# A fused local-attention and gated-MLP kernel on one core: the fourth unit in Strassen's stays, joined groups for it, softmax steps on GpSimd

## The chip, the cores and the metric

One core of a Trainium2 chip runs the whole program: TensorE (PE in the profile; PEld its weight loads), VectorE (DVE), ScalarE (ACT), GpSimd (POOL) and SyncE (SP), whose queue issues all of this kernel's DMAs. The metric is the device time in microseconds of one launch; lower is better.

## The reference

```python
q, k, v: (4, 8, 768, 64) float32      # batch, heads, sequence, head dim
scores = q @ k.T / 8
is_global = pos_k < n_global          # n_global = 8
is_local  = 0 <= pos_q - pos_k < n_local   # n_local = 96
dist = where(is_global & ~is_local, n_local, |pos_q - pos_k|)
scores = where(is_global | is_local, scores - slopes[h] * dist, -1e9)
a = exp(scores - max(scores))
a = a / (sum(a) + 1e-9)
x = (a @ v)                           # -> (3072 tokens, 512)
out = ((x @ w_a) * (x @ w_b)) @ w_out # w_a, w_b: (512, 1536); w_out: (1536, 512)
```

Each query sees at most 96 local keys and 8 global ones. The MLP has two first layers that are multiplied with each other, and a second layer.

## The kernel before

**Units, head pairs, feature pairs.** The 3072 tokens are six units of 512 tokens (0 to 5). A unit's attention is done in four head pairs of two heads ("granules", `granule_ops`, L648), each with four blocks of 128 queries. The 1536 features are six feature pairs (0 to 5) of 2 x 128 features. Each unit must meet each feature pair: 36 unit-and-pair passes of the MLP.

**Precision.** Every float32 operand of the MLP is split into a high and a low half in fp32r (`hh`/`hl`, `split`, L520), and each product is three matmuls: high x high, high x low, low x high. The weights arrive as raw words and are first converted (`to32`, L452: two ACT and four DVE operations on 128x512 a piece, six pieces a feature pair).

**Plain and Strassen.** `project_plain` (L1035) makes a pair's first layers of a unit with four products of 12 matmuls, 512 columns wide. `project` (L1095) does the same by Strassen's scheme with seven products of 12 matmuls, 256 wide; it needs sums and differences of the weight blocks (`convert`, L542, which writes them to DRAM, and `load_w`, L579, which reads and splits them) and of the blocks of X (`forms`, L906: four subtractions and seven splits; the plain `plain_forms`, L967, has four splits). The second layer (`back`, L1164, matmuls L1178) is 24 matmuls of 512 columns into four banks `acc` either way.

**Stays.** Only some feature pairs' weights fit in SBUF at a time. `STAYS` (L49) is the list of stays: which pairs are resident, which units come past in which order, and whether the stay is plain. `PASSES` (L57) is that list flattened. When the unit changes, the four `acc` banks are evicted and added to the unit's partial sums in DRAM (`evict`, L1195), and the next unit's X is loaded (`load_x`, L954) and put in forms, unless it has just come out of the attention.

**Attention of a granule.** PE makes the scores (L709, small 64x64 tiles), DVE adds the mask and reduces the minimum (L677), ACT takes exp and the sums (L693), DVE adds 1e-9 to the sums (L772) and takes reciprocals (L779), DVE or ACT scales (L792, L789), DVE transposes in 32x32 blocks (L808), a DMA writes the result to DRAM (`mir`) and eight DMAs bring it back rearranged as `px` and `py` (`carry`, L856), and PE makes the values (L341, or L322 in joined groups). Unit 0 (`DIRECT`) transposes on PE instead (L826, L827). There is one buffer each of `px`, `py` and `tt`, two of `t`, `vt` and `qk`.

Three ways exist to place the values. Unit 0 makes them at once. Units in `LAGGED` (1, 2, 3) make them after the next granule's scores, as a group of 32 matmuls of their own, and the scores in two groups of 24. Units in `JOINED` (4, 5) make all 48 score matmuls of a granule and the values of the granule before it (64 matmuls on 64x64 tiles, `parts`, L313) in one uninterrupted group on PE (`joined`, L726), which takes four PSUM banks. `NEAR` (0 to 3) are the units whose x is written straight into the tile X; the others' goes to DRAM through `vt` and is loaded when its pass comes.

**The order.** All operations go into a planner (`Schedule`, L160 on): each has a due time, costs per engine (`pe=`, `dve=`, `act=`, `pool=`), what it reads and writes, and the order of each engine's queue is fixed at build time by a list schedule over these. `SPANS` (L58) says over which stretch of passes (as positions in `PASSES`) a unit's attention is spread, `CONV` (L60) the same for the conversion of a feature pair's weights to Strassen's forms. Engines work through their queues in order, so an operation that waits holds up what stands behind it.

**The start.** `build` (L1535) loads the token counts, the table of positions and the first two granules' q and k, computes a flag, branches on it (the other side is a general, slow path that does not run here) and enters the planned program, whose first DVE work turns the table into distances and then into one mask per head (`masks`, L592).

## Time and profile before

| what | us |
|---|---|
| median of 3 runs | 723.44 |
| lowest and highest of them | 718.98, 724.59 |
| the profiled execution | 722.86 |
| its span, from first to last instruction | 721.0 |
| granted TensorE clock, mean | 0.990 |

The profiled execution is the one that all rows below come from. The span is what the rows show; 1.86 us lie around it. Rows of groups give the line of the kernel, the engine, the operation, output and input tiles with their sizes, the count, the time in which at least one of them ran, the mean length of one in ns, the idle time of the engine just in front of them, and what ended it. Rows of windows give a stretch of the span and each engine's busy time in it with the number of instructions, then the granted clock, the busy share of the 16 DMA engines and GB/s. Rows of the chain give start, length and work of what each step of the chain that ended last waited for.

### The profile page before, as it was taken

To read this page: it belongs to the slowest core of one execution; us is meant where nothing else is said; L and a number is where in the kernel's file an instruction comes from. 1 tells how busy PE (TensorE), PEld (TensorE's weight loads), DVE (VectorE), ACT (ScalarE), POOL (GpSimd) and SP (SyncE) were. 2 spreads that over 40 slices of the span, in tenths; PEclk is the share of its full clock that TensorE was granted. 3 is DMA by queue.
4 is the path that set the end of the run, shared out by engine and by line. 5 is a ranking of instruction groups with operands and counts; after the bars stand their busy time and mean duration, and the time that the engine had idled before them with its cause. 6 is when DMAs were issued, how large, how long until landed. Compare 5 with 4: busy or idle time off the path is not lost.

```text
span 721.0 us, 15565 instructions
## 1 busy us (share of the span) xinstructions
PE 685.9 (95%) x5808; PEld 602.3 (84%) x5808; DVE 581.6 (81%) x1552; ACT 384.9 (53%) x988; POOL 1.8 (0%) x8
## 2 busy tenths in 40 slices
PE   5598999999999999999999999999999999999995
PEld 4487877777777888888999998999898999999994
DVE  7999897878697776899899997999988558646652
ACT  5988675845565674566554546566434434424220
POOL 1000000000000000000000000000000000000000
PEclk9889999999999999999999999999999999999998
DMA  8547888998989997776786888748893423533121
GB/s 299 190 165 284 252 270 294 314 287 285 293 295 293 264 322 250 255 243 213 260 295 234 302 262 282 261 161 275 292 293 142 132 81 97 160 117 103 59 75 63
DMA packets 67910, 162.43 MB, mean 225 GB/s; under 512 B 8433, under 2 KB 21873, under 8 KB 66033
## 3 DMA queue, kind: packets, MB, share of 16 engines
q1 hardware_dynamic: 67824, 161.34, 67.7%
q8 instruction: 48, 0.79, 0.4%
q14 instruction: 38, 0.30, 0.1%
HBM read 110.45 MB, written 50.86 MB: 224 GB/s over the span
## 4 chain that ended last, share of the span: by engine, by line
PE 70%; DVE 13%; DMA 10%; ACT 4%; issue 2%; SPq 0%; ACTq 0%; DVEq 0%
PE acc L1178 22%; PE al L1001 16%; PE ga L1001 12%; PE ps L709 4%; DMA wr<-wts 3%; PE pa L341 3%; DMA qk<-qk 2%; DMA wl_A<-dw_A 1%; DVE t L677 1%; DVE tt L808 1%; DMA X<-dx 1%; DVE t L792 1%; DVE wm L495 1%; PE ps_al L322 1%; ACT wm L470 1%
## 5 line engine op out<-in xcount | busy, mean ns | idle before, releaser
L1178 PE MATMUL acc<-w_O,hh 128*128 128x512 f32 x576 | 197.0, 400 | 0.0
L1178 PEld LDWEIGHTS acc<-w_O,hh 128*128 128x128 f32 x576 | 108.3, 188 | 24.9 <-issue 1.5
L1178 PE MATMUL acc<-w_O,hl 128*128 128x512 f32 x288 | 113.7, 395 | 0.8 <-DVE hl L443 0.8
L693 ACT ACTIVATE t<-t,sm 128x168 f32<-128x168 f32 x192 | 81.1, 425 | 15.7 <-DVE sm L677 15.6
L1001 PE MATMUL al<-xf_T,w_S 128*128 128x256 f32 x576 | 76.7, 283 | 0.7 <-ACT s L433 0.7
L1001 PEld LDWEIGHTS al<-xf_T,w_S 128*128 128x128 f32 x576 | 72.4, 189 | 1.4 <-ACT s L433 0.9
L1178 PEld LDWEIGHTS acc<-w_O,hl 128*128 128x128 f32 x288 | 54.3, 188 | 10.8 <-DVE hl L443 1.4
L433 ACT CAST hh<-h 128x512 fp32r<-128x512 f32 (+1 forms) x61 | 36.0, 592 | 48.2 <-DVE h L443 23.6
L470 ACT ACTIVATE wm<-wr 128x512 f32<-128x512 f32 x54 | 36.2, 671 | 42.6 <-DMA wr<-wts 25.5
L709 PEld LDWEIGHTS ps<-qk 64*64 64x64 f32 x1056 | 32.8, 141 | 26.7 <-issue 14.0
L433 ACT COPY s<-al 128x512 f32<-128x512 f32 x44 | 25.7, 584 | 54.0 <-PE al L1001 53.8
L443 DVE TENSOR_TENSOR hl<-h,hh 128x512 fp32r<-128x512 f32 (+1 forms) x78 | 49.8, 644 | 4.9 <-ACT hh L433 4.5
L709 PE MATMUL ps<-qk 64*64 64x104 f32 (+2 forms) x1056 | 39.3, 276 | 14.5 <-DMA qk<-qk 7.1
L677 DVE CUSTOM_DVE_ANT_0 t<-ps,mask 128x168 f32<-128x168 f32 x176 | 48.6, 326 | 3.2 <-PE ps L709 3.0
L1110 DVE TENSOR_TENSOR s<-ga,s 128x512 f32<-128x512 f32 x48 | 32.8, 684 | 15.2 <-PE ga L1001 15.0
L808 DVE STREAM_TRANSPOSE tt<-t 128x512 f32<-128x512 f32 x80 | 40.9, 553 | 1.2 <-DMA mir<-tt 0.6
L1001 PE MATMUL ga<-xf_T,w_S 128*128 128x256 f32 x288 | 38.5, 283 | 1.1 <-DVE s L1110 1.0
L1001 PEld LDWEIGHTS al<-xf_B,w_A 128*128 128x128 f32 x288 | 37.5, 188 | 2.2
L505 ACT ACTIVATE wr<-wr 128x512 int32<-128x512 uint32 x54 | 36.1, 672 | 4.8 <-DVE xf_B L443 2.6
L1001 PE MATMUL ga<-xf_B,w_A 128*128 128x256 f32 x288 | 38.3, 283 | 0.3 <-DVE s L1110 0.3
L1001 PEld LDWEIGHTS ga<-xf_T,w_S 128*128 128x128 f32 x288 | 36.4, 188 | 2.6 <-DVE s L1110 2.0
L1001 PE MATMUL al<-xf_T,w_A 128*128 128x256 f32 x288 | 38.5, 283 | 0.1
(292 smaller groups left out, 1351.5 us busy)
## 6 DMA issues: line engine op xcount, KB each, us to landing
wr<-wts SPq DMA_DIRECT2D x54, 512.0 KB
qk<-qk SPq DMA_DIRECT2D x24, 720.0 KB
mir<-tt SPq DMA_DIRECT2D x20, 768.0 KB
vt<-vd SPq DMA_DIRECT2D x24, 512.0 KB
X<-dx SPq DMA_DIRECT2D x10, 1024.0 KB
part<-o SPq DMA_DIRECT2D x32, 256.0 KB
wl_S<-dw_S SPq DMA_DIRECT2D x32, 256.0 KB
px<-mir SPq DMA_DIRECT2D x60, 128.0 KB
```

The source lines that it names most:

```text
L341: self.main.nc.tensor.matmul(self.banks[0][64 * h : 64 * h + 64, o : o + P], self.vt[:lanes, v0 : v0 + 64], src[:, :, 2 * i + h], start=c ...
L433: self.nc.scalar.copy(out(), src())
L443: lambda e: self.nc.vector.tensor_tensor(out(), a(), b(), op=op),
L470: lambda e: nc.scalar.activation(m(), high().bitcast(F32), AF.Abs),
L505: lambda e: nc.scalar.activation(low(), low().bitcast(U32), AF.Copy, scale=2.0**-29),
L677: lambda e: nc.vector.tensor_tensor_reduce(t[:, i, h], bank[:, c0 : c0 + KW], self.mask[pair][:, h, kind], -0.125, 3.0e38, ALU.add, ALU.mi ...
L693: lambda e: nc.scalar.activation(t[:, i, h], t[:, i, h], AF.Exp, bias=sm[:, 0, j : j + 1], scale=-1.0, accum_out=sm[:, 1, j : j + 1],),
L709: nc.tensor.matmul(bank[64 * s : 64 * s + 64, c0 + c : c0 + c + w], qk[rows, q0 + 64 * s : q0 + 64 * s + 64], qk[rows, k0 + k : k0 + k + w ...
L808: nc.vector.transpose(dst[:, :, e0 : e0 + n], src[:, :, c0 : c0 + 32 * n].rearrange("p j (e k) -> p j e k", e=n),)
L1001: self.nc.tensor.matmul(bank[:, ab * HT : ab * HT + HT], w[:, a, (2 * ab + c) * P : (2 * ab + c) * P + P], x[:, b, c], start=first, stop=F ...
L1110: lambda e: nc.vector.tensor_tensor(s[:, :], bank[:, :], s[:, :], op=ALU.add),
L1178: self.nc.tensor.matmul(acc[i][:, :], a[:, rows], w[:, b], start=first and f == 0 and k == 0, stop=False, skip_group_check=True,)
```

## The change

There are five parts.

1. Unit 3 leaves the plain first stay. Its passes with feature pairs 0, 1 and 2 move into the later Strassen stays: (5, 2) then comes past units 3, 4, 5, and (0, 1) past 4, 5, 3, which makes unit 3 the last. The order of units now stands in `TURNS`, apart from `STAYS`. The spans of the attention and of the conversions are set anew, and unit 3 is no longer in `NEAR`.
2. Unit 3 moves from `LAGGED` to `JOINED`.
3. A joined group carries the values of the granule two before it (`BEHIND = 2`), across units. The loads of `px` and `py` for a granule (`carry`) are entered once the values before it have been taken. After the last granule the two remaining sets of values are made on their own.
4. The addition of 1e-9 moves to GpSimd; outside unit 0 it and the reciprocal are done once for all eight sums of a granule, not per half. On DVE the scaling of a half is one operation with a broadcast factor, not four.
5. The table of distances is computed in `build` ahead of the branch (`build_distances`), and the masks may be made by ACT or DVE, as the planner finds. Some of the planner's costs are changed (values 1900 to 2150, score groups 720 to 900, joined groups 2920 to 3150).

```diff
-STAYS = (
-    ((0, 1, 2), (0, 1, 2, 3), True),
-    ((3, 4), (3, 2, 1, 0), False),
-    ((5,), (0, 1, 2, 3), False),
-    ((5, 2), (4, 5), False),
-    ((3, 4), (5, 4), False),
-    ((0, 1), (4, 5), False),
-)
-PASSES = [(k, u) for k, stay in enumerate(STAYS) for u in stay[1]]
-SPANS = {1: (0.0, 0.6), 2: (0.85, 1.6), 3: (1.6, 2.6), 4: (3, 7), 5: (6.79, 11.5)}
-NEAR = (0, 1, 2, 3)
-CONV = {3: (1.72, 2.88), 4: (2.5, 3.5), 5: (4.39, 7), 2: (7.27, 10), 0: (10, 12.27), 1: (11.39, 14)}
+STAYS = (
+    ((0, 1, 2), True),
+    ((3, 4), False),
+    ((5,), False),
+    ((5, 2), False),
+    ((3, 4), False),
+    ((0, 1), False),
+)
+TURNS = ((0, 1, 2), (2, 1, 3, 0), (0, 1, 2), (3, 4, 5), (5, 4), (4, 5, 3))
+PASSES = [(k, u) for k, turn in enumerate(TURNS) for u in turn]
+SPANS = {1: (0.0, 0.6), 2: (0.85, 1.6), 3: (1.7, 3.5), 4: (3.4, 6.5), 5: (6.4, 9.8)}
+NEAR = (0, 1, 2)
+CONV = {3: (0.9, 2.2), 4: (1.7, 2.9), 5: (3.2, 6.0), 2: (5.5, 9.0), 0: (9.5, 13.0), 1: (11.0, 14.0)}
-LAGGED = (1, 2, 3)
-JOINED = (4, 5)
-JOINT = 2920.0
+LAGGED = (1, 2)
+JOINED = (3, 4, 5)
+JOINT = 3150.0
+BEHIND = 2
...
-        self.main.plan.op(self.due, self.emit, self.reads, self.claim(), pe=1900)
+        self.main.plan.op(self.due, self.emit, self.reads, self.claim(), pe=2150)
...
             op(
                 -1e5 + hd if p < 2 else 4000.0 + hd,
...
+                scale,
                 [full, self.slope],
                 [(self.mask[p], h)],
                 port=BOTH,
-                dve=dve(n, True),
+                dve=dve(n, True) + 60,
+                act=act(n) + 100,
             )
...
-            ahead = before
+            ahead = self.waiting.pop(0)[0] if len(self.waiting) == BEHIND else None
...
             if ahead:
                 ahead.take(due)
-            before = None
+                for _, carry in self.waiting[:1]:
+                    carry()
...
-            op(due, scores, [qk], ps, pe=720)
+            op(due, scores, [qk], ps, pe=900)
...
+        whole = u not in DIRECT
+
+        def sums(jw, js, k):
+            op(
+                due,
+                lambda e: nc.gpsimd.tensor_scalar_add(sm[:, 2, jw], sm[:, 1, jw], 1e-9),
+                [(sm, j) for j in js],
+                [(sm, ("d", k))],
+                pool=170,
+            )
+            op(
+                due,
+                lambda e: nc.vector.reciprocal(sm[:, 3, jw], sm[:, 2, jw]),
+                [(sm, ("d", k))],
+                [(sm, ("r", k))],
+                dve=100,
+            )
+
+        if whole:
+            sums(slice(0, 2 * NH), range(2 * NH), 0)
         for half in range(2):
...
-                lambda e, jw=jw: nc.vector.tensor_scalar_add(sm[:, 2, jw], sm[:, 1, jw], 1e-9),
...
-                lambda e, jw=jw: nc.vector.reciprocal(sm[:, 3, jw], sm[:, 2, jw]),
...
+            if not whole:
+                sums(jw, js, half)
...
-                    for j in js:
-                        nc.vector.tensor_scalar(
-                            flat()[:, j], flat()[:, j], sm[:, 3, j : j + 1], None, op0=ALU.mult
-                        )
+                    nc.vector.tensor_tensor(
+                        flat()[:, jw],
+                        flat()[:, jw],
+                        sm[:, 3, jw].unsqueeze(2).to_broadcast([P, 4, KW]),
+                        op=ALU.mult,
+                    )
...
-            op(due, norm, [(sm, ("r", half))], ts, port=BOTH, dve=4 * dve(KW, True), act=4 * (act(KW) + 100))
+            op(
+                due,
+                norm,
+                [(sm, ("r", 0 if whole else half))],
+                ts,
+                port=BOTH,
+                dve=dve(4 * KW),
+                act=4 * (act(KW) + 100),
+            )
...
+        then = Values(self, u, p, vt, px, py, x, d, due + VLAG)
         if u not in DIRECT:
-            self.carry(n, due, tt, px, py)
-
-        return Values(self, u, p, vt, px, py, x, d, due + VLAG)
+            carry = lambda: self.carry(n, due, tt, px, py)
+            if u in JOINED:
+                self.waiting.append((then, carry))
+                if len(self.waiting) == 1:
+                    carry()
+            else:
+                carry()
+        return then
...
+        if u == JOINED[-1]:
+            for k, (then, carry) in enumerate(self.waiting):
+                if k:
+                    carry()
+                then()
         return x
...
         nc.sync.dma_start(tiles["qk1"], a["qk"][0, 1])
+        build_distances(nc, nf, tiles["X"].rearrange("p a b -> p (a b)"))
         fast = nc.values_load(flag[0:1, 0:1], min_val=0, max_val=1)
...
+def build_distances(nc, nf, table):
+    ng, nl = nf[:, 0:1], nf[:, 1:2]
+    n = 2 * KW
+    rel, key, tmp = (table[:, i * n : i * n + n] for i in range(3))
+    v = nc.vector
+    v.tensor_scalar(tmp, rel, nl, BIG, op0=ALU.is_ge, op1=ALU.mult)
+    v.tensor_scalar(key, key, ng, BIG, op0=ALU.is_ge, op1=ALU.mult)
+    v.tensor_add(rel, rel, tmp)
+    v.tensor_scalar(key, key, nl, None, op0=ALU.add)
+    v.tensor_tensor(rel, rel, key, op=ALU.min)
```

More of the change, by code (lines that the diff above doesn't have):

```diff
@@ L399, in __init__ @@
         self.turns = 0
-        self.late = None
+        self.waiting = []
     def open(self):
@@ L598, in masks, with scale @@
         self.mask = [self.sbuf([P, 2, 2, KW], F32, f"mask{p}", f"mask{p}") for p in range(NPAIR)]
-        part = lambda i: full[:, :].rearrange("p a b -> p (a b)")[:, i * n : i * n + n]
-        rel, key, tmp = (lambda: part(0)), (lambda: part(1)), (lambda: part(2))
-        def steps(e):
-            v = nc.vector
-            v.tensor_scalar(tmp(), rel(), nl, BIG, op0=ALU.is_ge, op1=ALU.mult)
-            v.tensor_scalar(key(), key(), ng, BIG, op0=ALU.is_ge, op1=ALU.mult)
-            v.tensor_add(rel(), rel(), tmp())
-            v.tensor_scalar(key(), key(), nl, None, op0=ALU.add)
-            v.tensor_tensor(rel(), rel(), key(), op=ALU.min)
-        op(-2e5, steps, [], [full], port=BOTH, dve=3 * dve(n, True) + 2 * dve(n))
+        rel = lambda: full[:, :].rearrange("p a b -> p (a b)")[:, :n]
         for hd in range(H):
             p, h = divmod(hd, 2)
+            def scale(e, p=p, h=h, hd=hd):
+                dst = self.mask[p][:, h].rearrange("p a b -> p (a b)")
+                by = self.slope[:, hd : hd + 1]
+                if e == "act":
+                    nc.scalar.mul(dst, rel(), by)
+                else:
+                    nc.vector.tensor_scalar(dst, rel(), by, None, op0=ALU.mult)
             op(
                 -1e5 + hd if p < 2 else 4000.0 + hd,
-                lambda e, p=p, h=h, hd=hd: nc.vector.tensor_scalar(
-                    self.mask[p][:, h].rearrange("p a b -> p (a b)"),
-                    rel(),
-                    self.slope[:, hd : hd + 1],
-                    None,
-                    op0=ALU.mult,
-                ),
+                scale,
                 [full, self.slope],
@@ L769, in granule_ops @@
             jw = slice(4 * half, 4 * half + 4)
-            op(
-                due,
-                lambda e, jw=jw: nc.vector.tensor_scalar_add(sm[:, 2, jw], sm[:, 1, jw], 1e-9),
-                [(sm, j) for j in js],
-                [(sm, ("d", half))],
-                dve=70,
-            )
-            op(
-                due,
-                lambda e, jw=jw: nc.vector.reciprocal(sm[:, 3, jw], sm[:, 2, jw]),
-                [(sm, ("d", half))],
-                [(sm, ("r", half))],
-                dve=80,
-            )
+            if not whole:
+                sums(jw, js, half)
             flat = lambda: t[:, :].rearrange("p a b c -> p (a b) c")
@@ L892, in attention @@
             self.xsaved[u] = d
-        late, self.late = self.late, None
+        late = None
         for p in range(NPAIR):
             then = self.granule_ops(u, p, dues[p], x, d, late)
-            if u in LAGGED or u in JOINED:
+            if u in LAGGED:
                 late = then
-            else:
+            elif u not in JOINED:
                 then()
-        if late and u in JOINED and u + 1 in JOINED:
-            self.late = late
-        elif late:
+        if late:
             late()
+        if u == JOINED[-1]:
[3 more added lines that the diff above has]
+                then()
         return x
@@ L1261, in run @@
         for i in range(len(PASSES)):
-            fps, _, plain = STAYS[PASSES[i][0]]
+            fps, plain = STAYS[PASSES[i][0]]
             times.append(times[-1] + len(fps) * (fpt + (more if plain else 0.0)) + share[i])
@@ L1280, in run @@
             t = times[i]
-            fps, _, plain = STAYS[stay]
+            fps, plain = STAYS[stay]
             if i and PASSES[i - 1][1] != u:
@@ L1287, in run @@
                     xf[u] = self.load_x(u, t - 7000.0)
-            elif i and STAYS[PASSES[i - 1][0]][2] and not plain:
+            elif i and STAYS[PASSES[i - 1][0]][1] and not plain:
                 xf[u] = self.forms(u, t - 7000.0, x)
```

3 lines of the change are left out of this document (1 added, 2 removed).

## The prediction

> **What bounds the kernel now.** I read the page first, then the windows by stage, then the chain, then PE's waits, part by part.
>
> ```profile
> span 721.0 us, 15565 instructions
> PE 685.9 (95%) x5808; PEld 602.3 (84%) x5808; DVE 581.6 (81%) x1552; ACT 384.9 (53%) x988; POOL 1.8 (0%) x8
> PE 70%; DVE 13%; DMA 10%; ACT 4%; issue 2%; SPq 0%; ACTq 0%; DVEq 0%
> ```
> ```profile
> core 0: us, PE busy (x) PEld busy (x) DVE busy (x) ACT busy (x) POOL busy (x), PEclk, DMA share, GB/s
> 0.00:60.00 60.00, 40.95 (x473) 34.61 (x473) 52.25 (x208) 45.41 (x147) 1.82 (x8) 0.91 0.65 222
> 60.00:240.00 180.00, 174.23 (x1544) 141.86 (x1543) 149.39 (x500) 114.87 (x345) 0.00 (x0) 1.00 0.89 287
> ...
> 300.00:540.00 240.00, 238.06 (x2288) 218.68 (x2287) 227.03 (x557) 131.97 (x323) 0.00 (x0) 1.00 0.77 261
> 540.00:721.00 181.00, 172.62 (x1168) 158.82 (x1166) 110.23 (x199) 60.17 (x107) 0.00 (x0) 0.99 0.32 103
> ```
> PE is the bound: outside the first 60 us and the tail it is hardly ever idle (174.23 of 180, 238.06 of 240). From 300 to 540 DVE is 95% busy (227.03 of 240) and PE still loses only 2 us, so a full DVE alone doesn't make PE wait, as long as the planned order is right. In the front (0 to 240) DVE is 84% busy (201.6 of 240) and the DMA engines 0.89 from 60 on. So the sum is one of PE's own work, plus what its waits become. "Busy" PE includes overlapping ends; the price of a block of matmuls is therefore taken from the chain, where pieces follow each other:
>
> ```profile
> 142.38 2.80 PE ga_0(0, 1)_1935 L1022 x12
> 147.99 1.91 PE pa L341 x32
> 149.90 2.99 PE ga_1(0, 1)_2017 L1022 x12
> 152.89 0.75 PE ps L709 x16
> 153.63 2.29 PE acc L1178 x9
> 386.90 1.44 PE al L1001 x12
> 388.34 5.58 PE acc L1178 x24
> ```
> ```profile
> 256.39 1.04 PE ps L709 x24
> 257.72 1.58 PE acc L1178 x6
> ```
> ```profile
> 406.77 1.04 PE ps L709 x24
> 409.65 2.98 PE acc L1178 x12
> ```
> Columns: start, length, work. A product of 12 matmuls is 2.80 in the plain form (512 wide) and 1.44 in Strassen's (256 wide); the second layer of a feature pair (`acc`, 24 matmuls) is 5.58 in both. The block behind a switch to attention's small tiles is longer than the same block elsewhere (2.99 against 2.80), and I count that against the switch.
>
> **Part 1: the fourth unit leaves the plain stay.** 36 feature-pair passes stay 36, but 3 of them (pairs 0, 1, 2 of unit 3) turn from plain to Strassen. Plain: 4 x 2.80 + 5.58 = 16.78. Strassen: 7 x 1.44 + 5.58 = 15.66. That is 1.12 each, 3 x 1.12 = **3.4 us off PE's path**.
>
> What it adds lies on other engines. Evictions and loads of weights keep their number (14 runs of passes with the same unit, 8 loads of a pair). Loads of X go from 10 to 11, sets of Strassen forms of X from 11 to 12, plain sets from 4 to 3.
>
> ```profile
> L443 DVE TENSOR_TENSOR xT<-X 128x512 f32<-128x512 f32 x22 | 15.0, 682 | 0.7 <-ACT X L433 0.4 <-DMA X<-dx 0.3
> L1110 DVE TENSOR_TENSOR s<-ga,s 128x512 f32<-128x512 f32 x48 | 32.8, 684 | 15.2 <-PE ga L1001 15.0
> L772 DVE TENSOR_SCALAR sm<-sm 128x4 f32<-128x4 f32 x48 | 7.5, 157 | 5.0 <-ACT t L693 4.9
> L779 DVE RECIPROCAL sm<-sm 128x4 f32<-128x4 f32 x48 | 8.2, 170 | 0.4
> L792 DVE TENSOR_SCALAR t<-t,sm 128x168 f32<-128x168 f32 x112 | 26.7, 301 | 0.1
> ```
> DVE: three more additions in each of 3 passes, 9 x 0.684 = 6.2; 11 subtractions for the new set less 4 of the plain one, 7 x 0.682 = 4.8; together +11.0. ACT gets the copies of those, about 3 x 2 + 3 more of its pieces, and is at 53%. The extra X load is hidden: its due time lies 14 us ahead of its pass and one took 7.63 (row below). Unit 3's x now leaves per head pair (four writes of 256 KB on SP's queue in place of one of 1 MB), so it needs no free X buffer. I cost all this at nothing; what hides it is the 300-to-540 row: PE waits 2 us beside a DVE at 95%.
>
> **Part 2: joined groups for unit 3, values two pairs back.** A pair of unit 3 now costs PE its values, 1.91 + (2.99 - 2.80) = 2.10, and two score groups of 0.75 + (2.29 - 9/24 x 5.58) = 0.95: 4.00. A joined group takes 409.65 - 406.77 = 2.88, and 0.19 of the 12 matmuls behind it (2.98 against 2.79): 3.07. One without values: 257.72 - 256.39 = 1.33 and 0.18: 1.51. Before: 4 x 4.00 + 7 x 3.07 + 1.51 + 2.10 (unit 5's last values) = 41.1. After, 12 joined groups of which the first two carry no values, and two values alone at the end: 10 x 3.07 + 2 x 1.51 + 2 x 2.10 = 37.9. **3.2 us off PE's path.** The loads of `px`/`py` for a pair now wait until the values before have been read, on SP's queue; behind them stand loads of weights and X. Before, the same loads waited for the same buffer one pair earlier, so I take the queue's waits as unchanged.
>
> **Part 3: attention of units 3 to 5 moves forward.** Unit 5 is due by pass 9.8 of 18 and used from pass 12; before, 11.5 and 13. At present its end is exactly on time:
>
> ```profile
> 530.47 1.94 PE pa L341 x32
> 533.04 3.47 DMA dx<-vt
> 536.88 7.63 DMA X<-dx
> 556.72 1.71 PE ga L1001 x12
> ```
> The values, the write, the load and DVE's forms (544 to 556) follow each other, and PE loses 1.71 - 1.44 = 0.3 us and a little ahead of it. **0.4 us** goes; late next is nothing that I can find behind 540, where DVE is at 61% (110.23 of 181).
>
> **Part 4: the start and GpSimd.**
>
> ```profile
> 1.03 0.29 POOL masks.py:199 TENSOR_SCALAR_AFFINE_SELECT ident<-ident 128x128 f32<-128x128 f32 x1
> 5.76 0.73 DVE L604 TENSOR_SCALAR X<-X,nf 128x336 f32<-128x336 f32 x1 [0.76 <-DVE flag L1531]
> 8.44 1.31 DVE L615 TENSOR_SCALAR mask<-X,slope 128x336 f32<-128x336 f32 x4
> 34.92 0.45 PE L826 MATMUL pt<-ident,t 128*104 128x128 f32 x1 [0.71 <-DVE t L792]
> ```
> The table of distances is computed ahead of the branch on `flag`, so the 0.76 us in which DVE waits around the branch may be covered: gain 0 to 0.76. Half of the first four masks may go to ACT, which waits then anyway: gain 0 to 0.65 of the 1.31. Against it: each sum + 1e-9 leaves DVE, and DVE's queue now waits for GpSimd in front of each reciprocal. No row shows such a hop. Its nearest rows are the 0.29 of GpSimd's select and the 0.17 of a step that it replaces: bounds -0.17 and +0.46 each. The first product waits behind a transpose that waits 0.71 us for just this chain (last row). I count two hops there: -0.3 to +0.9. The ends of the three, -1.7 and +0.9, lie about nothing; I take **0** and keep them.
>
> In DVE's own time, 48 adds go (7.5) and 28 of 48 reciprocals stay (8 halves of unit 0, 20 whole pairs; 3.4 of 8.2 goes): -10.9, against +11.0 in part 1. The scaling of a half becomes one operation of 672 elements; from the 0.682 of 512, 0.90 as an estimate, against 4 x 0.301 less their overlap: between -0.3 and 0, or on ACT as now for 20 halves. So DVE's total stays where it is, and its share rises by one point through a shorter span.
>
> **Sum.** -3.4 - 3.2 - 0.4 + 0 = -7.0. The profiled execution took 722.86 (span 721.0 and 1.86 around it), 0.58 under the median of 723.44. 722.86 - 7.0 = 715.9; rounded, **716**.
>
> **The rivals.** What can go wrong is in the front, where PE's waits are now. From 40 to 130 us PE's waits have eight rows, 8.1 us in all, of which the first and the last, and two of those behind 130:
>
> ```profile
> PE ps L709 <- ACT X L433: 2.3, 2, 1.5
> PE pa L341 <- DMA py<-mir: 0.4, 2, 0.2
> ```
> ```profile
> PE ga L1001 <- DVE s L1110: 1.3, 2, 1.0
> PE pa L341 <- DMA py<-mir: 0.9, 2, 0.6
> ```
> *The hops stall DVE's queue (0.20).* 16 of the 28 fall in units 0 to 2, where DVE is 84% busy. At 0.46 each, all paid by PE, 7.4 us: 723. For it: the queue is in order and already waits 4.9 us for ACT in front of these steps. Against it: the order is planned with a lag for GpSimd, and other work stands between.
>
> *The hops are longer, since an add waits out a DVE operation (0.03).* With one of 0.68 (the additions' row) in front of each, 16 x 1.14 = 18.3: 734. Nothing bears it out, as POOL does nothing behind the first 7 us. The Trainium skill, "SBUF — State Buffer", section "Who interferes with whom", speaks for it: an operation of VectorE with two SBUF inputs shares a read interface with GpSimd, and whoever comes first holds it for the whole instruction. By that rule the price would be up to these 734; no run here shows it yet.
>
> *The weights come too late: slower (0.10).* Strassen's products begin at 307.6 now (first row). Three plain passes go from in front of them (3 x 16.8), and some 14 us of attention: about three joined groups (6) stand there where unit 3 (16.0) and unit 4's first two groups (4.6) stood. They begin at about 243 then. Pairs 3 and 4 must be converted, written and read back as 18 pieces of 256 KB by then. Of the 54 pieces of raw weights, 31 were issued in the first 240 us (x10 up to 60, x21 up to 240), one more than the 30 that pairs 0 to 4 need; but of the 18 reads back only 2 (last row, 60 to 240).
>
> ```profile
> L1001 PE MATMUL al<-xf_B,w_A x288: 274/282/361, 307.6 to 692.9; 128*128 128x256 f32 x144
> ```
> ```profile
> wr<-wts SPq DMA_DIRECT2D x10, 512.0 KB
> wr<-wts SPq DMA_DIRECT2D x21, 512.0 KB
> wl_A<-dw_A SPq DMA_DIRECT2D x2, 256.0 KB
> ```
> 18 x 0.26 MB at 287 GB/s are 16.4 us. The engines have 0.11 x 180 = 20 us free there, and about one pair of unit 3 (2.7 MB, 9 us) moves out of that stage, so it fits. If none of it is hidden, PE waits 16.4 us at the first Strassen pass: 732. It ends slower than before once more than 7 us of the 16.4 show.
>
> *The front gets better (0.17).* Of DVE's 10.9 us some 6 fall in units 0 to 2, ahead of where anything is added, and unit 3 no longer crowds in: if half of the 8.1 goes, 712.
>
> **How the numbers follow.** The forecast has 0.50, with a range of its own of 711 to 720: waits of the front 5 us less to 4 more. A measurement of this kernel can tell about 1% from no change, 7.2 us: the bounds are 716.2 and 730.7. The forecast lies on the first of them, so half of its 0.50 counts as faster. Faster: 0.26 + 0.17 = 0.43. Within 1%: 0.24 + 0.20 = 0.44. Slower: 0.10 + 0.03 = 0.13. The range reaches from the better front (709: 712 less the 1.7 and some more of the waits) to the stalled queue with the +0.9 and some loads late (727); outside it lie 0.13 above and about 0.06 below.
>
> **What would show it.** Right: 9 plain passes (products of 512 columns down by a quarter), the first Strassen product near 243 us against 307.6, ten joined groups with 64 small value matmuls each at 2.9 us, 11 loads of X, and PE's waits between 40 and 130 near 8 us. Wrong: PE waiting for `xf` or `w_A` at the first Strassen pass (weights); reciprocals that wait for POOL by over 0.3 us each with PE's transposes behind them (hops); the first product later than 37 us; or a plain pass in the front stretched by more than 2 us over its 16.78 a pair and the attention in it.

## The result, and the profile after

| | before | after |
|---|---|---|
| median (lowest to highest), us, 4 runs each on one chip | 723.87 (718.98 to 724.59) | 732.00 (730.83 to 733.65) |
| the profiled execution, us | 722.86 | 730.83 |
| its span, us | 721.0 | 729.1 |
| granted TensorE clock, mean | 0.990 | 0.984 |

The ratio is 1.0129, with a 95% interval of 1.0079 to 1.0178: the changed kernel is slower by 1.3%. 716 was forecast.

The page of the changed kernel, the lines shown of before:

```profile
span 729.1 us, 15962 instructions
PE 686.2 (94%) x6012; PEld 607.4 (83%) x6012; DVE 583.1 (80%) x1424; ACT 393.3 (54%) x1010; POOL 12.2 (2%) x36
...
X<-dx SPq DMA_DIRECT2D x11, 1024.0 KB
```

And its windows by stage (columns as before: busy time and instructions of PE, PEld, DVE, ACT, POOL; granted clock; share of the DMA engines; GB/s):

```profile
0.00:60.00 60.00, 39.42 (x492) 32.14 (x492) 50.34 (x178) 48.63 (x159) 4.80 (x16) 0.94 0.65 217
60.00:240.00 180.00, 171.91 (x1470) 140.74 (x1466) 144.44 (x414) 110.56 (x320) 4.15 (x10) 0.97 0.85 280
240.00:300.00 60.00, 55.58 (x526) 48.79 (x524) 51.79 (x122) 35.66 (x96) 0.89 (x3) 0.97 0.83 264
300.00:540.00 240.00, 236.61 (x2298) 216.98 (x2297) 219.01 (x500) 135.30 (x329) 2.32 (x7) 1.00 0.78 262
540.00:729.10 189.10, 182.71 (x1240) 168.78 (x1238) 117.50 (x213) 63.18 (x112) 0.00 (x0) 0.99 0.35 112
```

The kernel before from 240 to 300 us:

```profile
240.00:300.00 60.00, 60.00 (x347) 48.33 (x346) 42.71 (x92) 32.51 (x70) 0.00 (x0) 1.00 0.81 270
```

DVE lost the instructions that were to go (1552 to 1424). It is less busy up to 240 us (194.8 against 201.6 us) and busier from 240 to 300 (51.8 against 42.7), where the Strassen stage now begins; over the whole it is as busy as before (583.1 and 581.6). PE stands idle longer in the front (8.1 of 180 us between 60 and 240, before 5.8) and, what busy time doesn't show, its clock there fell from 1.00 to 0.97.

TensorE's own work did shrink as planned. The first Strassen product of each pass, in the rows of that matmul, and the joined group in the chain:

```profile
L1023 PE MATMUL al<-xf_B,w_A x324: 274/283/388, 254.5 to 702.6; 128*128 128x256 f32 x162
```
```profile
402.11 1.04 PE ps L703 x24
...
404.99 1.58 PE acc L1200 x6
```

324 in place of 288 are 27 Strassen passes in place of 24, so 9 plain ones. A joined group still takes 404.99 - 402.11 = 2.88 us. The saving of 6.6 us of parts 1 and 2 is therefore there in PE's work, and some 15 us in which PE waits or runs at a lower clock have come on top. To place them I take each stage's length and deduct its matmuls at the spacing that they have when nothing holds them (0.2323 us for a 512-wide one, 0.1195 for a 256-wide one, attention groups as the prediction prices them):

| stage | before: length - products - attention = rest | after | more |
|---|---|---|---|
| to the first plain product | 35.7 | 36.7 | +1.0 |
| from there to the first Strassen product | 272.0 - 196.1 - 60.3 = 15.6 | 217.8 - 145.9 - 48.6 = 23.3 | +7.7 |
| from there to the last matmul | 405.0 - 380.3 - 20.5 = 4.2 | 467.8 - 427.1 - 28.8 = 11.9 | +7.7 |
| behind it | 8.4 | 6.8 | -1.6 |

Which waits they are, from PE's waits of the changed kernel from 36 to 130 us and from 130 to 720 (total, times, longest):

```profile
PE ps L703 <- DVE sm L671: 4.8, 5, 3.0
PE pa L343 <- DMA px<-mir: 2.2, 1, 2.2
PE pt L845 <- ACT t L792: 1.5, 1, 1.5
```
```profile
PE ga L1023 <- ACT s L435: 4.4, 4, 3.7
PE ga L1023 <- DVE s L1132: 2.1, 2, 1.1
```

These three of the front alone are 8.5 us, more than all eight rows of before from 40 to 130 (8.1): PE waits for the mask and reduction on DVE (L671), for `px` and for a scaling that now runs on ACT (L792). All rows of the changed kernel from 36 to 130 us come to 10.8 us. From 130 to 720 us they come to 9.6, and to 3.1 in before. The longest single wait lies at the start of the Strassen stage, 263 to 267 us. The timeline of ACT in it:

```profile
259.77 1.41 ACT L792 ACTIVATE t<-t,sm 128x168 f32<-128x168 f32 x4
265.24 0.62 ACT L435 CAST w_A<-wl_A 128x512 fp32r<-128x512 f32 x1 [4.06 <-DMA wl_A<-dw_A]
265.93 0.62 ACT L435 CAST w_S<-wl_S 128x512 fp32r<-128x512 f32 x1
266.45 0.58 ACT L435 COPY s<-ga 128x512 f32<-128x512 f32 x1
```

ACT stands before a cast of Strassen weights that have not arrived. The copy of `s`, which PE needs to get its bank back, reads a product that was done at 260.6; it stands two places behind in the same queue and starts at 266.45. PE doesn't wait for weights here; it waits for work that is queued behind work that waits for weights. The late weights thus do start this wait, by way of ACT. Their read was issued at 259.72 us. What stands ahead of it on SP's queue, which issues the transfers, and the longest row of that queue's waits from 252 to 260 us:

```profile
252.12 1.65 SPq L426 DMA_DIRECT2D px<-mir  x4
253.81 5.32 SPq L426 DMA_DIRECT2D py<-mir  x4
259.23 0.37 SPq L426 DMA_DIRECT2D dx<-vt  x1
259.72 0.36 SPq L426 DMA_DIRECT2D wl_A<-dw_A  x1
```
```profile
SPq L426 <- DMA wr<-wts: 3.9, 2, 1.9
```

The eight loads of `px` and `py` for a head pair of unit 3 take the queue from 252.1 to 259.1 us, 3.9 of them in waits for raw weights under way. In before no such loads were issued between 278 and 319 us, and the first Strassen product is at 307.6.

The second part of the loss is the clock. Windows of the changed kernel around three of its waits, each pair the wait and the stretch behind it:

```profile
56.00:60.00 4.00, 1.02 (x31) 0.84 (x26) 3.88 (x16) 3.11 (x10) 0.00 (x0) 1.00 0.87 228
60.00:63.40 3.40, 3.40 (x22) 3.28 (x18) 2.24 (x11) 2.39 (x12) 0.24 (x1) 0.50 1.01 398
...
104.00:107.70 3.70, 2.09 (x10) 1.20 (x8) 3.51 (x13) 3.55 (x12) 0.48 (x1) 1.00 0.84 243
107.70:114.50 6.80, 6.17 (x43) 5.62 (x44) 5.96 (x12) 4.00 (x10) 0.00 (x0) 0.50 0.80 220
...
263.10:267.10 4.00, 0.31 (x3) 0.02 (x1) 1.21 (x2) 1.79 (x4) 0.00 (x0) 1.00 0.81 274
...
268.20:271.60 3.40, 3.40 (x15) 3.11 (x15) 3.11 (x7) 0.62 (x1) 0.00 (x0) 0.50 1.03 418
```

With each wait comes a stretch of 3.4 or 6.8 us in which PE has half its clock; it begins between 0.5 us before PE works again (107.8 against 108.33) and 1.1 us after (268.2 against 267.1). In before this happened only at 23.9 and 34.1 us, in the start; here at 32.7 in the start, and at 60.0, 107.8 and 268.2 behind it. These last three are 13.6 us in all, worth at most half of that, 6.8 us, and counted in the two +7.7 above. Of the first +7.7, 2.7 are longer waits and at most 3.9 the clock (in that stage before had 5.2 us of half clock, the changed kernel 13.0); of the second, 6.5 are waits and at most 1.7 the clock. The Trainium skill, "TensorE: Matmul & The Clock Gate", section "Why this matters for your kernels", advises to leave no gap of more than about 3 us between bursts of matmuls. The trace agrees in kind, but the gaps here were 2.98, 2.18 and 3.69 us, so the two shorter ones are under that bound.

### The profile page after: what moved, and what is told of

It is laid out like the page before. It is cut to its first block, busy times and chain, and to the rows that moved or that the text cites. A ratio compares the mean times of both kernels' runs of the same rounds, so it can differ in the third digit from the quotient of the medians.

```text
span 729.1 us, 15962 instructions
## 1 busy us (share of the span) xinstructions
PE 686.2 (94%) x6012; PEld 607.4 (83%) x6012; DVE 583.1 (80%) x1424; ACT 393.3 (54%) x1010; POOL 12.2 (2%) x36
## 4 chain that ended last, share of the span: by engine, by line
PE 54%; DMA 21%; DVE 15%; ACT 5%; issue 2%; SPq 1%; POOL 0%; DVEq 0%; ACTq 0%
PE acc L1200 18%; PE al L1023 15%; PE ga L1023 12%; DMA wr<-wts 5%; PE ps L703 2%; DMA mir<-tt 2%; DMA wl_S<-dw_S 2%; DVE t L671 2%; DMA X<-dx 2%; DMA py<-mir 2%; DMA qk<-qk 2%; DMA px<-mir 2%; DVE tt L821 1%; ACT t L687 1%; PE pa L343 1%
## 5 line engine op out<-in xcount | busy, mean ns | idle before, releaser
L1200 PEld LDWEIGHTS acc<-w_O,hh 128*128 128x128 f32 x576 | 108.6, 189 | 23.9 <-issue 0.9
L1023 PE MATMUL al<-xf_T,w_S 128*128 128x256 f32 x648 | 86.5, 283 | 0.4 <-ACT s L435 0.4
L1023 PEld LDWEIGHTS al<-xf_T,w_S 128*128 128x128 f32 x648 | 81.6, 189 | 1.6 <-ACT s L435 1.0
L703 PE MATMUL ps<-qk 64*64 64x168 f32 (+2 forms) x1008 | 37.5, 275 | 13.7 <-DMA qk<-qk 7.4
L1132 DVE TENSOR_TENSOR s<-ga,s 128x512 f32<-128x512 f32 x54 | 37.1, 687 | 16.4 <-PE ga L1023 16.1
L671 DVE CUSTOM_DVE_ANT_0 t<-ps,mask 128x168 f32<-128x168 f32 x168 | 46.6, 328 | 3.9 <-PE ps L703 3.1
L1023 PE MATMUL ga<-xf_B,w_S 128*128 128x256 f32 x324 | 43.8, 285 | 4.4 <-ACT s L435 4.4
L1023 PEld LDWEIGHTS ga<-xf_B,w_S 128*128 128x128 f32 x324 | 40.8, 190 | 5.4 <-ACT s L435 5.4
L1023 PE MATMUL ga<-xf_T,w_S 128*128 128x256 f32 x324 | 43.2, 283 | 2.1 <-DVE s L1132 2.1
L1023 PE MATMUL al<-xf_T,w_A 128*128 128x256 f32 x324 | 44.1, 286 | 0.6 <-DVE s L1132 0.6
L1023 PEld LDWEIGHTS al<-xf_B,w_A 128*128 128x128 f32 x324 | 42.2, 189 | 2.9 <-DVE sm L671 0.5
L1023 PEld LDWEIGHTS ga<-xf_T,w_S 128*128 128x128 f32 x324 | 41.0, 189 | 3.5 <-DVE s L1132 2.9
L1023 PEld LDWEIGHTS al<-xf_T,w_A 128*128 128x128 f32 x324 | 41.6, 192 | 2.1 <-DVE s L1132 1.4
```

The lines of the kernel that those rows point to most:

```text
L671: lambda e: nc.vector.tensor_tensor_reduce(t[:, i, h], bank[:, c0 : c0 + KW], self.mask[pair][:, h, kind], -0.125, 3.0e38, ALU.add, ALU.mi ...
L703: nc.tensor.matmul(bank[64 * s : 64 * s + 64, c0 + c : c0 + c + w], qk[rows, q0 + 64 * s : q0 + 64 * s + 64], qk[rows, k0 + k : k0 + k + w ...
L1023: self.nc.tensor.matmul(bank[:, ab * HT : ab * HT + HT], w[:, a, (2 * ab + c) * P : (2 * ab + c) * P + P], x[:, b, c], start=first, stop=F ...
L1132: lambda e: nc.vector.tensor_tensor(s[:, :], bank[:, :], s[:, :], op=ALU.add),
L1200: self.nc.tensor.matmul(acc[i][:, :], a[:, rows], w[:, b], start=first and f == 0 and k == 0, stop=False, skip_group_check=True,)
```

## The experiments

Each run is compared with the kernel before on the same chip; medians are in us, ratios with their 95% interval. The median of before lay between 722.7 and 723.9 in all of them.

**Which part of the change costs the time?** First the turns and the joined groups, put back. `h1_old_turns` puts unit 3 back into the plain stay, lagged, with the old spans; `e3_lagged3` takes unit 3 out of the joined groups; `f3_before_turns` gives the kernel before the new turns, spans and conversion times and nothing else.

```diff
# h1_old_turns (and SPANS, NEAR, CONV as before)
-TURNS = ((0, 1, 2), (2, 1, 3, 0), (0, 1, 2), (3, 4, 5), (5, 4), (4, 5, 3))
+TURNS = ((0, 1, 2, 3), (3, 2, 1, 0), (0, 1, 2, 3), (4, 5), (5, 4), (4, 5))
# h1_old_turns and e3_lagged3
-LAGGED = (1, 2)
-JOINED = (3, 4, 5)
+LAGGED = (1, 2, 3)
+JOINED = (4, 5)
```

> The changed kernel with the old order of units, spans, conversions and unit 3 lagged as before; two-back values for units 4 and 5, GpSimd's additions, masks and planner costs stay new. PE's own work is that of before (6.5 us more than in the changed kernel). Theory 'crowded front' (the shorter plain stay packs attention, conversions and transfers, and PE waits): the waits go with it, 719 to 725 us. Theory 'softmax' (the hop to GpSimd and the scaling on ACT stretch the chain in units 0 to 2): the waits stay, 732 us or more. Theory 'joined' (two-back groups of unit 3 are at fault): also 719 to 725, told apart by the next run.

> The changed kernel with unit 3 in lagged groups again (its x still goes through DRAM); all else new. PE's own work rises by 3 us. Theory 'crowded front': the waits before the first Strassen product stay, 731 to 737. Theory 'joined': they go, 720 to 727. Theory 'softmax': 733 to 736.

> The kernel before with only the new order of units, spans and conversion times (unit 3 lagged, x through DRAM, values one pair back). PE's own work falls by 3.4 us. Theory 'crowded front' (the shorter plain stay brings its own waits): 722 to 730, with PE's waits ahead of the first Strassen product at least 4 us longer than before. Without such waits: 717 to 721.

| run | median (lowest to highest, runs) | ratio |
|---|---|---|
| h1_old_turns | 734.59 (731.98 to 738.56, 4) | 1.0150 [1.0088, 1.0212] |
| e3_lagged3 | 737.26 (736.18 to 741.62, 4) | 1.0197 [1.0140, 1.0253] |
| f3_before_turns | 747.04 (746.21 to 749.53, 4) | 1.0337 [1.0305, 1.0369] |

With parts 1 and 2 both undone the changed kernel is slower still, by 2.6 us (6.6 were forecast), with part 2 alone undone by 5.3 (3.2 forecast). The sign is that of the forecast, but the sizes are not in step. The 2.6 are no more than the error of such a median, as the control below shows, and each edit also makes a new order of the queues. The turns alone are no gain: f3's 747 lies outside both readings of its expectation (717 to 730). In its order PE waits late for a pair's `px` and for a form of X. That the values one pair back are the reason is not shown. PE's waits of f3 behind 130 us, and the window that they lie in, at half the clock:

```profile
PE pa L342 <- DMA px<-mir: 10.9, 1, 10.9
PE al L1002 <- ACT xf_B L434: 8.6, 1, 8.6
```
```profile
525.90:553.20 27.30, 9.59 (x56) 8.53 (x57) 10.51 (x20) 6.02 (x11) 0.00 (x0) 0.50 0.42 145
```

Between the first plain and the first Strassen product its rest, worked out as in the table of stages, is 15.4 us, that of before 15.6: with unit 3 lagged it isn't the turns that crowd the front. What remains are the softmax's steps, part 5 and the planner's prices. The masks and the table of part 5 were never put back alone.

```diff
# e1_add_dve; e2_softmax_old has this, e2b_norm_old and the old halves of the sums
-                lambda e: nc.gpsimd.tensor_scalar_add(sm[:, 2, jw], sm[:, 1, jw], 1e-9),
+                lambda e: nc.vector.tensor_scalar_add(sm[:, 2, jw], sm[:, 1, jw], 1e-9),
-                pool=170,
+                dve=70,
# e2b_norm_old
-                    nc.vector.tensor_tensor(... to_broadcast([P, 4, KW]), op=ALU.mult)
+                    for j in js:
+                        nc.vector.tensor_scalar(
+                            flat()[:, j], flat()[:, j], sm[:, 3, j : j + 1], None, op0=ALU.mult
+                        )
-                dve=dve(4 * KW),
+                dve=4 * dve(KW, True),
```

> The changed kernel with the addition back on VectorE, but still one sum for eight and one scaling operation a half. If the hop to GpSimd is what costs in the softmax steps: about as with all of them undone, 724 to 729. If it is the scaling that went to ACT, or the sum for the whole pair: 730 to 734.

> The changed kernel with the old softmax steps: additions on VectorE, sums and reciprocals per half, four scalings a half at the old planner price. Theory 'softmax': 719 to 726, and PE's waits for transposes and scores in the first 130 us fall from about 20 us to 10. Theories 'crowded front' and 'joined': 728 to 734.

> The changed kernel with the four scalings a half at their old planner price; GpSimd's addition and the one sum for eight stay. If the scaling (its price sends more of it to ACT, and ACT is then late for unit 0) is what costs: 724 to 729. If it is the hop: 730 to 734.

`f1_before_softmax` is the kernel before with the new softmax steps.

> The kernel before with the new softmax steps alone (addition on GpSimd, one sum for eight outside unit 0, one scaling operation a half at its new planner price); order of units, joined groups, masks and prices of the groups as before. Theory 'softmax': it loses in the front by itself what the changed kernel loses there, 729 to 736 us, with more of PE's waits and more of the lowered clock ahead of 130 us. Theory 'crowded boundary alone': 719 to 725.

| run | median (lowest to highest, runs) | ratio |
|---|---|---|
| e1_add_dve | 727.12 (722.76 to 731.53, 10) | 1.0050 [1.0018, 1.0082] |
| e2_softmax_old | 728.22 (723.72 to 732.48, 10) | 1.0060 [1.0029, 1.0091] |
| e2b_norm_old | 723.36 (721.13 to 727.12, 10) | 1.0004 [0.9977, 1.0032] |
| f1_before_softmax | 727.14 (723.11 to 733.59, 8) | 1.0083 [1.0050, 1.0117] |

All four are slower than before or equal to it, and they don't add up: the four old scalings alone give back 8.6 us, the add and the halves of the sums put back beside them make it 4.9 worse. GpSimd's add stays in e2b, which is level with before, so the hop isn't what costs the 8.6 us. Taken alone, e1 fell where the reading "hop" had put it (724 to 729), and e2 (728.2) and f1 (727.1) fell outside what the reading "softmax" had given them (719 to 726 and 729 to 736).

**A control.** An edit of one price by 10 ns, and the planner's prices of the score groups, values and joined groups put back together with the old softmax:

```diff
# n1_null
-JOINT = 3150.0
+JOINT = 3140.0
# e6_softmax_costs_old: e2_softmax_old and
-JOINT = 3150.0
+JOINT = 2920.0
-... self.claim(), pe=2150)
+... self.claim(), pe=1900)
-            op(due, scores, [qk], ps, pe=900)
+            op(due, scores, [qk], ps, pe=720)
```

> The changed kernel with one planner price moved by 10 ns (joined groups 3140 instead of 3150); the same work in a slightly different order. If the loss belongs to the change's content: 729 to 734. Theory 'luck of the order' (any new order moves the time by several us): it may come out anywhere from 718 to 738.

> The changed kernel with the old softmax steps and the old planner prices of the groups (values 1900, scores 720, joined 2920): the order of units, joined groups with values two back, and the masks are left of the change. If the new prices cost time: 716 to 723. If what is left of the loss lies at the boundary between the plain and the first Strassen stay: 725 to 731.

n1_null: 731.36 (722.95 to 737.38, 9 runs), 1.0090 [1.0039, 1.0141]. e6: 725.13 (715.69 to 729.58, 10 runs), 0.9982 [0.9941, 1.0024]. n1 kept the changed kernel's time, as expected if the loss belongs to the change's content. But its queues are those of the changed kernel until past the start of the Strassen stage, so it tests only what a new order does behind that. e6 lies at the edge of its second reading (725 to 731) and its runs spread over 14 us, so it doesn't settle whether the prices of the groups cost time. Runs of one program spread by up to 2% here, so I take a median of four as good to some 3 us, an estimate.

**The operation, or its price in the plan?** The scaling of a half can run on DVE or ACT, and the planner chooses by the price. The old price is four times the short form, some 620 ns; the new is one operation of 672 elements, some 770. `i1_tt_oldprice` keeps the one operation and plans it at the old price; `i2_ts_newprice` has the four operations at the new one.

```diff
# i1_tt_oldprice
-                dve=dve(4 * KW),
+                dve=4 * dve(KW, True),
```

> The changed kernel with its one scaling operation a half, but planned at the old price of four, so that every engine's queue has the same order as in the run with four operations at that price (723.4 us), and only the operation itself differs. Theory 'order' (the price moved the scaling of unit 0 to ACT, and the order that follows is the worse one): 720 to 726. Theory 'operation' (the broadcast multiplication itself costs, beside GpSimd): 729 to 734.

> The counterpart: four scaling operations, planned at the new price of one, so that all queues have the changed kernel's order (731.5 us) and only the operation differs. Theory 'order': 729 to 734. Theory 'operation': 720 to 726.

i1: **722.94** (720.89 to 728.19, 10 runs), 1.0006 [0.9976, 1.0036]. i2: **731.50** (728.26 to 734.64, 4 runs), 1.0125 [1.0087, 1.0163]. i2 has the changed kernel's queues, instruction by instruction but for the scaling itself, and i1 has those of e2b:

| | old price | new price |
|---|---|---|
| one operation | 722.9 (i1) | 732.0 (the changed kernel) |
| four operations | 723.4 (e2b) | 731.5 (i2) |

This settles it: which operation runs makes no difference that shows (0.5 us at most), and its price costs 8 to 9 us, through the plan alone. The price changes the order of PE's, ACT's, DVE's and SP's queues, and it lets ACT scale one half more (24 in place of 23).

**Where does the price act?** `k1` has the old price for unit 0 (four tiles, eight halves) alone, `k2` for all other units alone.

```diff
# k1_unit0_oldprice
-                dve=dve(4 * KW),
+                dve=4 * dve(KW, True) if u in DIRECT else dve(4 * KW),
```

> The changed kernel with the scaling priced for the order by the old sum (four times the short form) for unit 0's tiles alone, at the price of one broadcast operation for all others; the operations are those of the changed kernel. Theory (the price costs time because it puts unit 0's scaling on ACT in the start and the first passes, where ACT is full): no scaling on ACT before 60 us, first product as early as before (about 36 us), and nearly all of the 8.5 us between the two orders comes back: 722 to 725. Rival (the price costs time later, between 45 and 270 us, through the order on DVE and ACT there): the time stays at 729 to 733.

> The counterpart: the price of one broadcast operation for unit 0 alone, the old sum for all other units. Theory (it acts through unit 0): 729 to 733, with halves on ACT before 50 us. Rival (it acts later): 722 to 725. If both this and its counterpart land near 727, the price acts in both places.

k1: 724.57 (720.25 to 727.44, 12 runs), 1.0009 [0.9985, 1.0034]. k2: 737.62 (732.42 to 739.24, 6 runs), 1.0170 [1.0133, 1.0207]. It is unit 0's eight halves; that k2 is slower still than the changed kernel, and outside both its readings, stays open. The expectation of k1 was wrong in one thing: it too scales on ACT before 60 us. Here are these scalings in the changed kernel, then in k1 (count, least, median and longest ns, first and last start):

```profile
L792 ACT ACTIVATE t<-t,sm x16: 417/420/435, 16.5 to 47.3; 128x168 f32<-128x168 f32 x16
```
```profile
L792 ACT ACTIVATE t<-t,sm x12: 417/420/436, 32.9 to 47.8; 128x168 f32<-128x168 f32 x12
```

One half, the second of the first tile, moves between DVE (at 15 us) and ACT (at 16.5). Two more runs ask whether this half does it: `k5` forbids ACT for the first tile at the new price, `k7` is i1 with that half forced onto ACT.

```diff
# k5_first_dve
-                act=4 * (act(KW) + 100),
+                **({} if u in DIRECT and p == 0 else {"act": 4 * (act(KW) + 100)}),
# k7_half_act: i1_tt_oldprice and
-                dve=4 * dve(KW, True),
+                **({} if u in DIRECT and p == 0 and half else {"dve": 4 * dve(KW, True)}),
```

> The changed kernel with its own prices, but the first tile of unit 0 may be scaled on DVE alone: in the changed kernel its second half is scaled on ACT at 16.5 us, in the three versions at 723 to 725 on DVE at 15, and this is the only place in unit 0 where they differ. Theory (this one half on ACT, in front of the other work of ACT in the start, costs the 8.5 us): 722 to 726. Rival (where the half is scaled is only a mark of two orders, and the order that follows decides): the time is not tied to it, most likely still 727 to 735.

> The converse: the changed kernel planned at the old price, which takes about 723, but with the second half of unit 0's first tile scaled on ACT alone. Theory (the half on ACT costs the time): 729 to 733. Rival (it is the order that follows): 721 to 727.

k5: 724.87 (722.16 to 729.84, 12 runs), 1.0023 [0.9994, 1.0052]. k7: **718.50** (716.84 to 723.29, 12 runs), 0.9936 [0.9910, 0.9962]. The first agrees with the theory, the second refutes it: with the half on ACT at 16.4 us k7 is the fastest kernel of the study. So the half is one of the first places at which the two plans part, and the order that follows makes the time. k7 leaves one rival: the planner gave back others of unit 0's halves to DVE, so that ACT scales two of them in the start and not four. k8, a run of the next part, speaks against this rival: ACT scales five halves there, the first at 16.2 us, and k8 takes 724.6. The scalings of k7, then of k8:

```profile
L792 ACT ACTIVATE t<-t,sm x8: 419/422/438, 16.4 to 43.1; 128x168 f32<-128x168 f32 x8
```
```profile
L792 ACT ACTIVATE t<-t,sm x20: 417/420/435, 16.2 to 49.2; 128x168 f32<-128x168 f32 x20
```

k7's windows beside the changed kernel's, from 36 to 130 and from 130 to 260 us, first the changed kernel, then k7, then the kernel before from 36 to 130:

```profile
36.00:130.00 94.00, 84.56 (x796) 73.88 (x796) 81.35 (x237) 65.62 (x187) 3.45 (x6) 0.93 0.75 236
130.00:260.00 130.00, 127.70 (x1094) 101.36 (x1094) 102.79 (x291) 80.16 (x236) 2.35 (x8) 1.00 0.87 285
```
```profile
36.00:130.00 94.00, 85.52 (x859) 73.93 (x858) 85.50 (x261) 67.75 (x200) 2.59 (x6) 0.98 0.82 257
130.00:260.00 130.00, 127.08 (x1060) 101.47 (x1058) 100.96 (x277) 78.62 (x226) 2.53 (x8) 1.00 0.89 289
```
```profile
36.00:130.00 94.00, 85.87 (x861) 74.54 (x860) 84.01 (x287) 66.91 (x196) 0.00 (x0) 0.97 0.79 257
```

The first Strassen products of k7:

```profile
L1023 PE MATMUL al<-xf_B,w_A x324: 274/282/386, 248.0 to 690.0; 128*128 128x256 f32 x162
```

From 36 to 130 us k7 gets more work through PE, DVE, ACT and the DMA engines than the changed kernel, about as much as before did: 859 matmuls against 796, clock 0.98 against 0.93, DVE 4 us and ACT 2 us more, the DMA engines 0.82 against 0.75. Its Strassen stage begins at 248.0 in place of 254.5, and from there to the end of the span it takes 716.7 - 248.0 = 468.7 in place of 474.6.

**A better order on purpose.** Since late transfers stood in front of several waits, `k3` lets the plan count 3300 ns in place of 2300 after a transfer, with e2b's scaling; `k8` does it to the changed kernel itself; `w4` is k3 with due times and spans moved as well.

```diff
# k3_dmalag, k8_after_lag, w4_spaced
-LAGS = {"pe": 200.0, "act": 270.0, "dve": 230.0, "pool": 290.0, "dma": 2300.0}
+LAGS = {"pe": 200.0, "act": 270.0, "dve": 230.0, "pool": 290.0, "dma": 3300.0}
# w4_spaced, among others
-SPANS = {1: (0.0, 0.6), 2: (0.85, 1.6), 3: (1.7, 3.5), 4: (3.4, 6.5), 5: (6.4, 9.8)}
+SPANS = {1: (0.0, 0.6), 2: (0.89, 1.29), 3: (1.59, 3.61), 4: (3.19, 6.66), 5: (6.4, 9.8)}
-LOADLEAD = 7790.0
-VLAG = 13280.0
+LOADLEAD = 10064.8
+VLAG = 10980.0
...
```

> The changed kernel with the four scalings at the old price, and planned with 3.3 us instead of 2.3 from a DMA's issue to its use, with due times of attention, conversions and the first products moved to suit; the work is the same. If transfers that land later than planned are what gives the gain back: 712 to 719. If not: 721 to 727.

> The changed kernel with four scalings at the old price, and in the plan the lag counted after a transfer 3300 ns in place of 2300, nothing else. Theory (the spaced version gains because the queues' order allows for later transfers): about half or more of its gain over the kernel before, 719 to 722. Rival (the gain came from the moved due times and turns' spans, not from the lag): 723 to 726, as with the old lag.

> The changed kernel unaltered but for one number of the plan: 3300 ns in place of 2300 counted after a transfer. Theory (a plan that allows for later transfers is better in itself): about 2 us or more below the changed kernel as with the old price of the scaling, where it brought 2 us, so 730 or less, and 723 or less if the unit's order is also put right. Rival (what counts is which of many orders comes out, and the lag is one more throw): anywhere in the spread that the orders of this work have shown, 718 to 738, with no tie to the lag.

| run | median (lowest to highest, runs) | ratio |
|---|---|---|
| w4_spaced | 721.00 (714.47 to 725.60, 10) | 0.9940 [0.9904, 0.9976] |
| k3_dmalag | 721.49 (718.24 to 724.09, 12) | 0.9957 [0.9933, 0.9981] |
| k8_after_lag | 724.64 (721.32 to 729.08, 12) | 1.0006 [0.9979, 1.0033] |

The lag brought 1.9 us to e2b's order and 7.4 to the changed kernel's. Two trials are in favour of it and none against; that it helps in itself, and isn't only another throw, they don't show.

Orders of nearly the same work beside each other (e2b, w4 and k3 scale with four operations), each with its median, the first Strassen product and what follows it to the end of the span. The last two columns are of the profiled execution alone, which took 726.3 for i1 and 719.4 for k3 and lies within 1.2 us of the median for the others:

| order | median us | first Strassen product | rest |
|---|---|---|---|
| with the waits of before (forecast) | 716 | 246 | 468 |
| k7_half_act | 718.5 | 248.0 | 468.7 |
| w4_spaced | 721.0 | 252.0 | 468.2 |
| k3_dmalag | 721.5 | 249.4 | 468.2 |
| i1_tt_oldprice | 722.9 | 255.6 | 468.9 |
| e2b_norm_old | 723.4 | 251.3 | 470.7 |
| k1_unit0_oldprice | 724.6 | 251.4 | 471.0 |
| k8_after_lag | 724.6 | 258.7 | 463.6 |
| k5_first_dve | 724.9 | 251.1 | 471.7 |
| n1_null | 731.4 | 254.0 | 475.5 |
| the changed kernel | 732.0 | 254.5 | 474.6 |
| k2_rest_oldprice | 737.6 | 259.7 | 475.0 |

The 246 is before's 35.7 + 145.9 + 48.6 + 15.6, from the table of stages. In k8, 18 matmuls of the second layer (4.2 us) run ahead of the first Strassen product that run behind it in the changed kernel. The 19 us between the fastest and the slowest order are nearly three times what the change saves. No single wait carries them. Between k7 and the changed kernel 6.5 us lie ahead of the first Strassen product and 5.9 behind it. A split by one execution is good to some 4 us only: i1 and e2b, which queue alike, have their first Strassen product 4.3 us apart. Against the changed kernel all of i1's gain lies behind that product, and 3.2 us of e2b's 7.1 ahead of it.

## Why the prediction was wrong

**Parts 1 and 2 (-3.4 and -3.2): right as prices of PE's work.** The counts are as forecast, and the joined group takes 2.88 as priced. The runs that undo them were slower, but they don't show the size, since each has an order of its own. k7, the best order, is 5.2 us below before on the same chip; other orders of the old work at their best weren't tried, so that the 5.2 aren't shown to be the saving. The sentence about part 2, "I take the queue's waits as unchanged", held only for the joined groups themselves: none of their value matmuls (L324, from 230.6 us on) waited. But their loads of `px` and `py` stood ahead of the weights of the first Strassen pass on SP's queue, and PE's wait of 3.7 us followed. Whether the wait would go with them wasn't tested: k7 has the same loads there (245.5 to 251.5 us) and no wait of PE for such a copy over 1.1 us. The `px` that came 2.2 us late at 106 us, with 6.8 us at half the clock, is that of a lagged granule, which part 2 doesn't touch.

**Part 3 (-0.4): not shown.** The Strassen stage as a whole lost 7.7 us; a gain of 0.4 can't be seen in it.

**Part 4 (0): this is the step that failed.** I priced the scaling as an operation ("between -0.3 and 0, or on ACT as now for 20 halves") and costed it at nothing. As an operation that was right: i1 and e2b don't differ (0.85 us measured, 0.90 estimated). But the same line of the diff changes what the planner believes, and I read the prices in the diff only as a list of numbers. With the plan the order of the queues changes, and that cost 9.1 us with one operation (i1 against the changed kernel) and 8.1 with four (e2b against i2). The error is larger than this line: "I cost all this at nothing; what hides it is the 300-to-540 row" took the waits of one order as a property of the work. They belong to the order, and every part of the change made a new one. The 6.9 us that remain between i1 (722.9) and the forecast are waits of that kind too, at least in part, as k7, which has i1's work in another order, gets 4.4 of them back. Where the other 2.5 us are stays open. Part 5, whose masks the forecast took as a gain of 0 to 0.65 us, is in all these runs and was never undone alone.

**The range.** 709 to 727 was made from bounds of the costs of operations. What an order can do was in it as "waits of the front 5 us less to 4 more". Orders of nearly the same work have spread over 718 to 738.

**The rivals.** *The hops stall DVE's queue* (723): no. In the changed kernel DVE waited for GpSimd 2.8 us in 4 places of 28, and e2b has the hops without the loss. *The add waits out a DVE operation* (734): the mechanism is there, the price isn't. GpSimd's adds, and the longest of them beside DVE's timeline:

```profile
L767 POOL TENSOR_SCALAR sm<-sm x28: 220/236/849, 11.3 to 447.9; 128x8 f32<-128x8 f32 x20, 128x4 f32<-128x4 f32 x8
```
```profile
45.17 0.85 POOL L767 TENSOR_SCALAR sm<-sm 128x4 f32<-128x4 f32 x1 [3.14 <-ACT t L687]
```
```profile
45.27 0.67 DVE L497 SCALAR_TENSOR_TENSOR wm<-wr,wm 128x512 int32<-128x512 int32 x1
46.05 0.18 DVE L774 RECIPROCAL sm<-sm 128x4 f32<-128x4 f32 x1
```

The add ends 0.08 us after DVE's two-input operation (45.94 and 46.02) and takes 0.85 in place of 0.236. That is what the rule of the Trainium skill cited in the prediction says, and the trace agrees as to the delay. Who came first these rows don't show, as the add's record starts 0.10 us ahead of that operation's; at 75.4 us the order is that of the rule (DVE's operation from 75.38 to 76.07, the add from 75.41 to 76.17). But such delays are few: 5 of the 28 adds took 0.69 us or more, and all 28 together 3.8 us more than at 0.236 each. *The weights come too late* (732): the time was near, but by luck. At the first Strassen pass PE didn't wait for weights itself; late weights cost it 3.7 us, not 16.4, through a copy queued behind their cast on ACT, and in k1, k3 and k7 no wait for such a copy is longer than 1.1 us. *The front gets better* (712): no, it got worse by 7.7.

**The signs named ahead.** The first product came at 36.7, inside the 37 set as a bound. The first Strassen product came at 254.5 in place of "about 243" (246 by the stages' table): 8.5 us of the miss could be read there, 6.5 behind it. The stage of the plain passes was stretched, by 7.7 us in all.

## What to carry to other kernels

Where a planner orders the queues, a price in the source is an edit of the program: changing it for the eight halves of unit 0 (0.85 us each on DVE) moved the time by 7.4 us (k1), more than the work that the whole change saved. So part the two before judging a change: run the new operation at the old price and the old operation at the new one, and try several orders of the new work before calling it faster or slower. And the waits of a profile are not a constant to add saved work to; where PE is already 95% busy, a new order can easily add more to them than the saving, and the range has to say so.

## What the runs showed of the hardware

In the changed kernel waits of PE of 2.2 to 3.7 us came with 3.4 or 6.8 us at half the granted clock, worth at most 1.7 or 3.4 us, so that a short wait can cost as much again. In f3 two waits of 10.9 and 8.6 us came with 27.3 us at half the clock. A lowered clock isn't the whole account: behind 40 us k3 had none and took 721.5, f1 none and 727.1, w4 10.2 us of it and 721.0, k1 as much and 724.6, n1 as much and 731.4, the changed kernel 13.6 us and 732.0.
